# Moving the gate's clip of MLP 2 from VectorE to ScalarE, and half of the late w_out slices from MLP 2 into MLP 1

## The chip, the core and the metric

The kernel runs on one core of one Trainium2 chip. The metric is the time of one execution on the device in microseconds; lower is better. The core's engines are TensorE (PE: matmuls; PEld: its weight loads), VectorE (DVE), ScalarE (ACT), GpSimd (POOL) and SyncE (SP), whose queue issues all DMAs here. Each engine works through its own instructions in program order, so an instruction that waits holds up all that stand behind it.

## What is computed

Windowed attention feeds two MLPs in a row. The attention output becomes `x` with 3072 rows (tokens) and 512 columns; then

```python
def _moe_ref(x, w_in, w_out):            # MLP 1
    h = x @ w_in                         # 3072x512 @ 512x2048
    g = h - np.tanh(h)
    return g @ w_out                     # 2048x512

def _moe2_ref(x, w_in, w_out):           # MLP 2
    h = x @ w_in
    g = np.where(h >= 1, h, np.where(h <= -1, 0.0, (h + 1) ** 2 / 4))
    return g @ w_out
```

The weights arrive as 64-bit floats; the kernel rounds them to 32 bits itself, from their low and high words.

## The kernel before, in words

**Precision and rate.** Each factor is split into a high part (ACT copies it to `fp32r`, which rounds) and a low part (DVE subtracts the high part): `split_to`, lines 205 to 207. A product is then three matmuls (high by high, high by low, low by high), 128x128 by 128x512 each.

**MLP 1** is 96 steps (`NS`): 6 blocks of 512 tokens by 16 slices (`FC`) of 128 hidden columns. A step has 12 matmuls into `h` (`hidden`, line 464), the gate (`gate`: ACT Tanh, line 474, and DVE subtract, line 475) and, 16 steps behind (`LAG`), 12 matmuls into `acc` (`output`, `second`, line 499). The loop over steps `i` also calls what three tables hold for that step: `before` and `rounds` ahead of the step's matmuls, `behind` after its gate. `at_step` fills these tables by hand-set step numbers. The order in which the engines see the work is the order of these calls; nothing reorders it.

**The weights of MLP 2** are prepared inside MLP 1 by those tables: a slice is loaded into a `stage` tile (SP, line 121), turned into magnitude and low word on ACT (`round_act`, lines 133 and 136), put together by four DVE instructions (`round_rest`, lines 142, 143, 151 and 156), split (one ACT, one DVE instruction) and stored to DRAM (`wout`, two DMAs, line 244). Sixteen slices of `w_in` and the first eight of `w_out` (`EARLY_OUT`) are done in MLP 1, the `w_out` slices with one load tile (`stage3`) and one raw tile (`prep0`). The other eight (`LATE_OUT`) are done in MLP 2.

**MLP 2** is 24 calls of `quad(n)`: 3 superblocks of 1024 tokens by 8 pairs of hidden slices. A quad forms four 128x512 tiles of `h` with seven products (`mult`, 6 matmuls each, line 616) in place of eight, in the order 1, 2, 6, 5, 7, 4, 3, in two PSUM tiles: `qa` (bank `a`; two buffers in turn) and `qb` (banks `b` and `c`; one buffer, so that product 2 of a quad waits until the last gate of the quad before has read it). Partial sums leave `qa` by an ACT copy (`u`, line 632) ahead of the next product into it. The four gates (`gate2`, 96 in all) take `h` from a DVE add (line 643; one of the four reads `qa` directly). Line 646 clips to [-1, 1] on DVE, line 647 squares `0.5 t + 0.5` on ACT, and a last DVE instruction (`end`, line 650), put off to the next `gap`, takes the maximum with `h`.

Between the products stand four places, `gap(n, 0)` to `gap(n, 3)`. In each one output step of 12 matmuls is done: first the 17 left over from MLP 1 (`acc`; four each in quads 0 and 1, three each in quads 2 to 4, by `OLD_GAPS`), then those of MLP 2 (`acc_n`). `gap` splits the factors of the next output step as well (`ghi`, `glo`, `whi`, `wlo`). A quad has thus 90 matmuls with four output steps and 78 with three.

**The late slices before.** In quads 0 to 3, `late_out` does two slices per quad: round the first after gap 0, split it after gap 1, round the second after gap 2, split it after gap 3. The loads stand in the same quads: the first at the quad's start (line 730), the second after the first's split (line 756). In quad 3 four loads of activations for the next superblock (`x_load`, line 532) and eight loads of prepared weights (`load_out`, line 600) are issued ahead of the first. All these DMAs are in SP's one queue, with the `in<-win` loads (line 590) that feed the products.

Of the kernel before, what the change touches and what calls it, by code (L numbers as in the profile page):

```python
# [9 lines left out]
F32R = mybir.dt.float32r  # L10
# [3 lines left out]
AF = mybir.ActivationFunctionType  # L14
ALU = mybir.AluOpType
# [16 lines left out]
FC = DFF // 128  # L32
# [27 lines left out]
HALF = FC // 2  # L60
NSB = NB // 2
STREAM_IN, STREAM_OUT = 10, 8


OLD_GAPS = [(0, 1, 2, 3)] * 2 + [(0, 1, 2)] * 3

SPACE_A = (3, 4)
# [8 lines left out]
def tile_memory_attention_two_mlps(  # L76
# [9 lines left out]
    nc = tc.nc  # L86
# [13 lines left out]
    def slot(tag, name, dtype=F32):  # L100
        return slots.tile([128, 512], dtype, tag=tag, name=name)
# [3 lines left out]
    half = const.tile([128, 1], F32, name="half")  # L105
# [9 lines left out]
    def load_weights(phase, which, fc, tag=None):  # L115
        src = ((w1_in, w1_out), (w2_in, w2_out))[phase][which]
        if tag is None:
            tag = f"stage{loaded[0] % STAGES}"
            loaded[0] += 1
        stage = wide.tile([128, 512, 2], I32, tag=tag, name=f"stage{phase}{which}_{fc}")  # L120
        nc.sync.dma_start(out=stage, in_=src[fc])
        stage_t[phase, which, fc] = stage
# [3 lines left out]
    def round_act(phase, which, fc, part=None, tag=None):  # L126
        stage = stage_t[phase, which, fc]
        low, high = stage[:, :, 0], stage[:, :, 1]
        if part != 1:
            t = slot(tag or f"raw{which}_{fc}", f"raw{phase}{which}_{fc}")  # L130
            raw_t[phase, which, fc] = t

            nc.scalar.activation(out=t, in_=high.bitcast(F32), func=AF.Abs)
        if part != 0:

            nc.scalar.activation(out=low, in_=low.bitcast(U32), func=AF.Copy, scale=2.0 ** -29)
# [88 lines left out]
        for i, t in enumerate(parts_t.pop((q, m))):  # L225
            nc.sync.dma_start(out=win_d[q][:, 2 * m + i, :], in_=t.bitcast(F32))

    def prep_out_load(fc):
        load_weights(1, 1, fc, "stage3")

    def prep_out_act(fc):
        round_act(1, 1, fc, tag="prep0")

    def prep_out_rest(fc):
        round_rest(1, 1, fc)

    def prep_out_split(fc):
        hi, lo = slot("prep4", f"prepoh{fc}", F32R), slot("prep5", f"prepol{fc}", F32R)
        split_to(raw_t.pop((1, 1, fc)), hi, lo)
        parts_t["out", fc] = hi, lo  # L240

    def prep_out_store(fc):
        for i, t in enumerate(parts_t.pop(("out", fc))):
            nc.sync.dma_start(out=wout_d[fc][:, i, :], in_=t.bitcast(F32))
# [57 lines left out]
    scale = 1.0 / float(D) ** 0.5  # L302
# [147 lines left out]
    NS = len(steps)  # L450
# [186 lines left out]
    def gate2(n, r, c, src, plus=None):  # L637
        sb, q = n // HALF, n % HALF
        tag, g = take(f"g2_{n}_{r}{c}")
        gate_t[sb, r, q + c * HALF] = tag, g  # L640
        h = src
        if plus is not None:
            nc.vector.tensor_tensor(out=g, in0=src, in1=plus, op=ALU.add)  # L643
            h = g
        ttag, t = take(f"t2_{n}_{r}{c}")
        nc.vector.tensor_scalar(out=t, in0=h, scalar1=-1.0, scalar2=1.0, op0=ALU.max, op1=ALU.min)  # L646
        nc.scalar.activation(out=t, in_=t, func=AF.Square, scale=0.5, bias=half)  # L647

        def end():
            nc.vector.tensor_tensor(out=g, in0=h, in1=t, op=ALU.max)  # L650
            give(ttag)

        later.append(end)
# [64 lines left out]
    def quad(n):  # L718
        sb, q = n // HALF, n % HALF
        nxt = sb + 1  # L720
        more = nxt < NSB
        if more and q == HALF - 5:
            x_load(nxt)
        if n == 4:
            spare.extend(f"prep{i}" for i in range(6))
        if n == 3:
            for _ in range(STREAM_OUT // 2):
                load_out([spare.pop(0) for _ in range(2)])
        if n < 4:
            prep_out_load(LATE_OUT[2 * n])  # L730
        a = ps_h.tile([128, 512], F32, tag="h", name=f"qa{n}")
        pair = ps_a.tile([128, 2, 512], F32, tag="a", name=f"qb{n}")
        b, c = pair[:, 0, :], pair[:, 1, :]

        def mult(i, bank, first):
            if q == 0 or i not in (1, 2):
                xc[i] = xnext[i]
            product(n, i, bank, first)

        def then(i):  # L740
            if more and q == HALF - 1:
                x_split(nxt, i)

        def late_out(part):
            if n < 4:
                i, p = divmod(part, 2)
                fc = LATE_OUT[2 * n + i]
                if p == 0:
                    if i:
                        prep_out_store(LATE_OUT[2 * n])  # L750
                    prep_out_act(fc)
                    prep_out_rest(fc)
                else:
                    prep_out_split(fc)
                    if i == 0:
                        prep_out_load(LATE_OUT[2 * n + 1])

        mult(1, a, True)
        t1, u1 = take_copy(f"u1_{n}", a)
        mult(2, b, True)  # L760
        gate2(n, 0, 0, b, u1)
        give(t1)
        if q == 0:
            x_split(sb, 4) if sb == 0 else None
        gap(n, 0)
        late_out(0)
        if q == 0:
            x_split(sb, 3)
        if more and q == HALF - 4:
            x_sums(nxt, 0)  # L770
        if more and q == HALF - 2:
            x_split(nxt, 1)
        if more and q == HALF - 1:
            x_sum_last(nxt)
        mult(6, a, False)
        t2, u2 = take_copy(f"u2_{n}", a)
        mult(5, c, True)
        then(6)
        gap(n, 1)
        late_out(1)  # L780
        then(5)
        if more and q == HALF - 3:
            x_sums(nxt, 1)
        mult(7, a, False)
        t3, u3 = take_copy(f"u3_{n}", a)
        gate2(n, 1, 1, c, u3)
        give(t3)
        gap(n, 2)
        late_out(2)
        then(7)  # L790
        if more and q == HALF - 2:
            x_split(nxt, 2)
        mult(4, a, False)
        gate2(n, 1, 0, a)
        mult(3, c, False)
        gate2(n, 0, 1, c, u2)
        give(t2)
        gap(n, 3)
        late_out(3)
        if n < 4:  # L800
            prep_out_store(LATE_OUT[2 * n + 1])
        then(4)

    def out_fc_list(a, b):
# [2 lines left out]
    EARLY_OUT, LATE_OUT = out_fc_list(0, HALF), out_fc_list(HALF, FC)  # L807


    before, rounds, behind = {}, {}, {}  # L810

    def at_step(events, i, f, *args):
        assert i >= 0
        events.setdefault(int(i), []).append((i, f, args))


    for t in range(PER, NG + 1):
        k = t - PER
# [31 lines left out]
    for i, fc in enumerate(EARLY_OUT):  # L850
        p = PREP_IN + 5 + PREP_IN_EVERY * i
        at_step(before, p - 2, prep_out_load, fc)
        at_step(before, p, prep_out_act, fc)
        at_step(rounds, p, prep_out_rest, fc)
        at_step(before, p + 1, prep_out_split, fc)
        at_step(before, p + 2, prep_out_store, fc)


    def x_first():
# [28 lines left out]
    for j in range(PER):  # L888
        w = 0, 0, j
# [128 lines left out]
```

## Time and profile before

| what | value |
|---|---|
| median of 3 runs | 1146.48 us (1146.0 to 1146.83) |
| the profiled execution's own time | 1147.7 us |
| its span, first to last instruction | 1145.9 us |
| PE, DVE, ACT, POOL busy | 97%, 66%, 49%, 4% |
| mean granted TensorE clock over the span | 0.99 of full speed |
| DMA | 202.67 MB, mean 177 GB/s |
| MLP 1 steps, then quads of MLP 2 | quad 0 begins at 576.85 us |

The profile is one execution; its own time is 1.2 us above the median of the runs. Times in the rows count from the first instruction. "Idle before" is time in which an engine had nothing to run, and the name behind the arrow is what ended it. The granted clock is given as a share: 1.00 is 2.4 GHz, 0.50 is 1.2 GHz.

### The profile page before, as it was taken

The numbers are of one execution on the slowest core, as the hardware profiler recorded it, in microseconds if no ns is written. First come the engines' busy times: TensorE is split into PE (matmuls) and PEld (weight loads), VectorE is DVE, ScalarE is ACT, GpSimd is POOL, SyncE is SP. The second block draws the span as 40 slices with busy tenths as digits, with TensorE's granted clock in tenths as the row PEclk, the third lists the DMA queues.
The fourth block names the chain that finished last, engine by engine and source line by source line (L and its number), as shares of the span: only waits on it lengthen the run. The fifth ranks groups of instructions, "written<-read, shape, count | busy, mean of one in ns | idle before, by whom it ended". The sixth has DMA issues, their size and how long they took to land.

```text
span 1145.9 us, 20140 instructions
## 1 busy us (share of the span) xinstructions
PE 1107.9 (97%) x7799; PEld 897.1 (78%) x7799; DVE 759.2 (66%) x1340; ACT 556.0 (49%) x964; POOL 42.6 (4%) x38
## 2 busy tenths in 40 slices
PE   7899999999999999999999879999999999999998
PEld 3677888888888888888877658888888888888876
DVE  4799987887887887788567665565355564453522
ACT  3566665655656555566445443443334443333321
POOL 1132221000000000000000000000000000000000
PEclk9999999999999999999999989999999999999999
DMA  9996653626555454352244765657766557566364
GB/s 222 240 249 185 180 144 84 193 77 197 156 154 175 131 146 148 117 169 92 84 137 154 246 216 184 195 184 238 241 217 229 178 197 232 198 197 211 110 221 147
DMA packets 159648, 202.67 MB, mean 177 GB/s; under 512 B 61760, under 2 KB 86336, under 8 KB 159552
## 3 DMA queue, kind: packets, MB, share of 16 engines
q1 hardware_dynamic: 159552, 201.38, 56.5%
q8 instruction: 62, 1.02, 0.4%
q14 instruction: 34, 0.28, 0.1%
HBM read 165.68 MB, written 35.65 MB: 176 GB/s over the span
## 4 chain that ended last, share of the span: by engine, by line
PE 84%; DVE 7%; DMA 4%; ACT 3%; SPq 1%; issue 1%; DVEq 0%; ACTq 0%
PE h L464 23%; PE acc_n L499 22%; PE acc L499 19%; PE qa L616 9%; PE qb L616 7%; PE a L368 1%; DMA start<-qkv_t 1%; PE a L312 1%; DMA in<-win 1%; DVE g L650 1%; PE b L354 1%; DMA stage<-w_out 1%; DVE g L643 1%; DVE t L646 1%; DVE glo L207 1%
## 5 line engine op out<-in xcount | busy, mean ns | idle before, releaser
L207 DVE TENSOR_TENSOR glo<-g,ghi 128x512 fp32r<-128x512 f32 x192 | 132.6, 690 | 156.7 <-ACT ghi L206 105.7
L499 PE MATMUL acc_n<-ghi,out 128*128 128x512 f32 x768 | 194.2, 391 | 1.6 <-ACT yn L509 1.6
L499 PEld LDWEIGHTS acc_n<-ghi,out 128*128 128x128 f32 x768 | 143.3, 188 | 34.8 <-ACT yn L509 5.4
L206 ACT ACTIVATE ghi<-g 128x512 fp32r<-128x512 f32 x192 | 119.7, 624 | 80.9 <-PE acc L499 46.4
L616 PE MATMUL qa<-xc,in 128*128 128x512 f32 x576 | 148.0, 392 | 9.8 <-ACT u L632 9.7
L647 ACT ACTIVATE t<-t,half 128x512 f32<-128x512 f32 x96 | 69.5, 724 | 145.3 <-DVE t L646 145.0
L175 DVE TENSOR_TENSOR wlo<-raw,whi 128x512 fp32r<-128x512 f32 x192 | 134.7, 702 | 4.7 <-ACT whi L168 4.7
L616 PEld LDWEIGHTS qa<-xc,in 128*128 128x128 f32 x576 | 108.6, 189 | 33.9 <-ACT u L632 11.5
L168 ACT ACTIVATE whi<-raw 128x512 fp32r<-128x512 f32 x192 | 120.6, 628 | 23.9 <-PE acc L499 16.5
L643 DVE TENSOR_TENSOR g<-qb,u 128x512 f32<-128x512 f32 x72 | 49.7, 690 | 101.6 <-ACT u L632 77.6
L474 ACT ACTIVATE g<-h 128x512 f32<-128x512 f32 x96 | 57.2, 596 | 121.4 <-PE h L464 88.0
L616 PE MATMUL qb<-xc,in 128*128 128x512 f32 x432 | 111.3, 393 | 3.7 <-DVE g L643 3.7
L499 PE MATMUL acc<-ghi,whi 128*128 128x512 f32 x384 | 110.7, 403 | 2.5 <-ACT y L509 1.5
L499 PE MATMUL acc<-ghi,wlo 128*128 128x512 f32 x384 | 106.3, 391 | 0.4 <-DVE wlo L175 0.2
L499 PE MATMUL acc<-glo,whi 128*128 128x512 f32 x384 | 105.7, 389 | 0.0
L499 PE MATMUL acc_n<-glo,out 128*128 128x512 f32 x384 | 105.5, 389 | 0.0
L464 PE MATMUL h<-xh,whi 128*128 128x512 f32 (+2 forms) x392 | 105.4, 391 | 0.0
L632 ACT ACTIVATE u<-qa 128x512 f32<-128x512 f32 x72 | 42.8, 595 | 127.9 <-PE qa L616 127.9
L464 PE MATMUL h<-xl,whi 128*128 128x512 f32 (+2 forms) x392 | 103.9, 387 | 0.2 <-DVE xl L399 0.2
L464 PE MATMUL h<-xh,wlo 128*128 128x512 f32 (+2 forms) x392 | 103.7, 386 | 0.0
L616 PEld LDWEIGHTS qb<-xc,in 128*128 128x128 f32 x432 | 81.6, 190 | 21.9 <-DVE g L643 5.0
L475 DVE TENSOR_TENSOR g<-h,g 128x512 f32<-128x512 f32 x96 | 66.1, 688 | 47.8 <-ACT g L474 47.6
(89 smaller groups left out, 1327.3 us busy)
## 6 DMA issues: line engine op xcount, KB each, us to landing
out<-wout SPq DMA_DIRECT2D x192, 256.0 KB, 3.0
in<-win SPq DMA_DIRECT2D x168, 256.0 KB, 3.6
stage<-w_in SPq DMA_DIRECT2D x32, 512.0 KB, 5.2
stage<-w_out SPq DMA_DIRECT2D x32, 512.0 KB, 4.2
k<-qkv_t SPq DMA_DIRECT2D x80, 128.0 KB, 4.8
v<-qkv_t SPq DMA_DIRECT2D x80, 128.0 KB, 3.4
win<-preph SPq DMA_DIRECT2D x32, 256.0 KB, 3.0
yd<-y SPq DMA_DIRECT2D x24, 256.0 KB, 2.7
```

The source lines that it names most:

```text
L168: nc.scalar.activation(out=hi, in_=r, func=AF.Copy)
L175: nc.vector.tensor_tensor(out=lo, in0=r, in1=hi.bitcast(F32), op=ALU.subtract)
L206: nc.scalar.activation(out=hi, in_=src, func=AF.Copy)
L207: nc.vector.tensor_tensor(out=lo, in0=src, in1=hi.bitcast(F32), op=ALU.subtract)
L464: nc.tensor.matmul(hp, w[:, kc * 128:(kc + 1) * 128], x[:, kc, n0:n1], start=j == 0 and kc == 0, stop=j == 2 and kc == KC - 1,)
L474: nc.scalar.activation(out=g, in_=hp, func=AF.Tanh)
L475: nc.vector.tensor_tensor(out=g, in0=hp, in1=g, op=ALU.subtract)
L499: nc.tensor.matmul(acc_t[dm], w[:, dm * 128:(dm + 1) * 128], g, start=first and j == 0, stop=last and j == 2,)
L616: nc.tensor.matmul(bank, w[:, k * 128:(k + 1) * 128], z[k], start=first and j == 0 and k == 0, stop=j == 2 and k == 1, skip_group_check=True,)
L632: nc.scalar.activation(out=t, in_=bank, func=AF.Copy)
L643: nc.vector.tensor_tensor(out=g, in0=src, in1=plus, op=ALU.add)
L647: nc.scalar.activation(out=t, in_=t, func=AF.Square, scale=0.5, bias=half)
```

## The change

Three things change, in the code below.

1. **The gate.** DVE's clip is gone. ACT does Relu of `0.5 h + 0.5`, then Square, and the last DVE instruction does `max(min(t, 1), h)` in one.
2. **Four late slices move into MLP 1.** Slices 0 to 3 of `LATE_OUT` are rounded at steps 88, 90, 92 and 94 and split one step later, with loads two steps ahead, each into a `stage` tile of its own, and with two sets of prepared tiles in turn.
3. **The other four stay in quads 0 to 3, one per quad:** rounded after gap 0, split after gap 2, stored after gap 3. Their loads are issued at steps 94 (three) and 95 (one), ahead of quad 0.

```diff
+LATE_ALONE = 4
@@ gate2
-        nc.vector.tensor_scalar(out=t, in0=h, scalar1=-1.0, scalar2=1.0, op0=ALU.max, op1=ALU.min)
-        nc.scalar.activation(out=t, in_=t, func=AF.Square, scale=0.5, bias=half)
+        nc.scalar.activation(out=t, in_=h, func=AF.Relu, scale=0.5, bias=half)
+        nc.scalar.activation(out=t, in_=t, func=AF.Square)
         def end():
-            nc.vector.tensor_tensor(out=g, in0=h, in1=t, op=ALU.max)
+            nc.vector.scalar_tensor_tensor(out=g, in0=t, scalar=1.0, in1=h, op0=ALU.min, op1=ALU.max)
@@ quad
-        if n < 4:
-            prep_out_load(LATE_OUT[2 * n])
...
         def late_out(part):
-            if n < 4:
-                i, p = divmod(part, 2)
-                fc = LATE_OUT[2 * n + i]
-                if p == 0:
-                    if i:
-                        prep_out_store(LATE_OUT[2 * n])
-                    prep_out_act(fc)
+            i = n + LATE_ALONE
+            if i < HALF:
+                fc = LATE_OUT[i]
+                if part == 0:
+                    prep_out_act(fc, i)
                     prep_out_rest(fc)
-                else:
-                    prep_out_split(fc)
-                    if i == 0:
-                        prep_out_load(LATE_OUT[2 * n + 1])
+                elif part == 2:
+                    prep_out_split(fc, i)
+                elif part == 3:
+                    prep_out_store(fc)
@@ the tables of MLP 1
+    for i, fc in enumerate(LATE_OUT):
+        p = NS - FC + 8 + 2 * i
+        if i < LATE_ALONE:
+            at_step(before, p - 2, prep_out_load, fc, i)
+            at_step(before, p, prep_out_act, fc, i)
+            at_step(rounds, p, prep_out_rest, fc)
+            for k, f, args in ((1, prep_out_split, (fc, i)), (2, prep_out_store, (fc,))):
+                at_step(before if p + k < NS - 1 else behind, min(p + k, NS - 1 + 0.1 * k), f, *args)
+        else:
+            at_step(behind, NS - 2 if i < 2 * LATE_ALONE - 1 else NS - 1, prep_out_load, fc, i - LATE_ALONE)
```

TensorE's instructions stand in the same order in both kernels. Three places on other engines follow, before and now. Lines from 65 on have moved: 121, 133, 168, 206, 244, 590, 600, 632, 643 of before are 122, 134, 169, 207, 246, 592, 602, 634, 645 now.

SP's queue in quad 3, before; the `out` rows are the last two of eight loads of prepared weights, behind four of activations:

```order
L600 DMA out_0_3_0_7695<-wout_109 128x512
L600 DMA out_0_3_1_7696<-wout_109 128x512
L121 DMA stage_7_7699<-w_out 128x1024
L590 DMA in_3_7717<-win_96 128x512
L590 DMA in_4_7719<-win_96 128x512
L590 DMA in_5_7768<-win_96 128x512
L590 DMA in_6_7770<-win_96 128x512
L121 DMA stage_15_7796<-w_out 128x1024
L244 DMA wout_107<-prepoh_7792 128x512
L244 DMA wout_107<-prepol_7793 128x512
```

The same place now:

```order
L602 DMA out_0_3_0_7712<-wout_109 128x512
L602 DMA out_0_3_1_7713<-wout_109 128x512
L592 DMA in_3_7732<-win_96 128x512
L592 DMA in_4_7734<-win_96 128x512
L592 DMA in_5_7783<-win_96 128x512
L592 DMA in_6_7785<-win_96 128x512
L592 DMA in_0_7851<-win_97 128x512
L592 DMA in_1_7853<-win_97 128x512
L592 DMA in_2_7865<-win_97 128x512
L246 DMA wout_115<-prepoh_7841 128x512
L246 DMA wout_115<-prepol_7842 128x512
```

The two loads of raw `w_out` slices (`stage`) are gone from this quad; they stand at the end of MLP 1.

ACT in quad 3 before, from the copy of the quad's first product (`u_3`) to the copy ahead of its fifth, with the rounding of a late slice (`raw`, `stage`) between:

```order
L632 ACTIVATE u_3_7709<-qa_7701 128x512
L647 ACTIVATE t_3_00_7723<-t_3_00_7723,half 128x512
L206 ACTIVATE ghi_7726<-g_6880 128x512
L168 ACTIVATE whi_91_7730<-raw_11_2355 128x512
L133 ACTIVATE raw_7_7747<-stage_7_7699 128x512
L136 ACTIVATE stage_7_7699<-stage_7_7699 128x512
L632 ACTIVATE u_3_7760<-qa_7701 128x512
```

The same place now:

```order
L634 ACTIVATE u_3_7724<-qa_7716 128x512
L648 ACTIVATE t_3_00_7738<-g_3_00_7736,half 128x512
L649 ACTIVATE t_3_00_7738<-t_3_00_7738 128x512
L207 ACTIVATE ghi_7741<-g_6906 128x512
L169 ACTIVATE whi_91_7745<-raw_11_2355 128x512
L134 ACTIVATE raw_15_7762<-stage_15_7137 128x512
L137 ACTIVATE stage_15_7137<-stage_15_7137 128x512
L634 ACTIVATE u_3_7775<-qa_7716 128x512
```

Relu and Square stand where Square stood; the rounding is in the same place, of a slice that was loaded at step 95.

DVE in quad 2 before, from the second gate's add (`g_2_11`) to the ends of the last two gates; the next quad's product 2 waits for the add `g_2_01`:

```order
L643 TENSOR_TENSOR g_2_11_7605<-qb_7501,u_2_7603 128x512
L646 TENSOR_SCALAR t_2_11_7607<-g_2_11_7605 128x512
L207 TENSOR_TENSOR glo_7611<-g_6832,ghi_7610 128x512
L175 TENSOR_TENSOR wlo_90_7616<-raw_10_2233,whi_90_7614 128x512
L650 TENSOR_TENSOR g_2_11_7605<-g_2_11_7605,t_2_11_7607 128x512
L142 TENSOR_SCALAR raw_14_7633<-raw_14_7633 128x512
L143 TENSOR_SCALAR raw_14_7633<-raw_14_7633 128x512
L151 SCALAR_TENSOR_TENSOR raw_14_7633<-stage_14_7595,raw_14_7633 128x512
L156 ISA raw_14_7633<-stage_14_7595,raw_14_7633 128x1024
L646 TENSOR_SCALAR t_2_10_7651<-qa_7500 128x512
L643 TENSOR_TENSOR g_2_01_7662<-qb_7501,u_2_7559 128x512
```

The same place now:

```order
L645 TENSOR_TENSOR g_2_11_7631<-qb_7533,u_2_7629 128x512
L208 TENSOR_TENSOR glo_7637<-g_6847,ghi_7636 128x512
L176 TENSOR_TENSOR wlo_90_7642<-raw_10_2233,whi_90_7640 128x512
L652 SCALAR_TENSOR_TENSOR g_2_11_7631<-t_2_11_7633,g_2_11_7631 128x512
L208 TENSOR_TENSOR prepol_7658<-raw_7_7578,prepoh_7657 128x512
L645 TENSOR_TENSOR g_2_01_7683<-qb_7533,u_2_7591 128x512
```

Two clips and the four roundings of the second slice are gone from between the two adds; one subtraction of the late slice's split (`prepol`) has come in.

## Rows read from the trace of the kernel before

**Rows 1.** Page, part 1: busy time of each engine, share, instructions.

```profile
PE 1107.9 (97%) x7799; PEld 897.1 (78%) x7799; DVE 759.2 (66%) x1340; ACT 556.0 (49%) x964; POOL 42.6 (4%) x38
```

**Rows 2.** Who PE waited for, whole span: us in total, times, longest.

```profile
PE qa L616 <- ACT u L632: 9.7, 3, 8.5
...
PE qb L616 <- DVE g L643: 3.7, 3, 2.2
```

**Rows 3.** Busy time by stretch (length, engines, clock, DMA): one step, quads 0 to 4.

```profile
565.97:571.41 5.44, 5.44 (x25) 4.50 (x24) 1.99 (x3) 1.87 (x3) 0.00 (x0) 1.00 0.01 3
576.85:600.11 23.26, 21.43 (x91) 16.58 (x90) 15.90 (x28) 12.30 (x22) 0.00 (x0) 1.00 0.54 169
600.11:623.03 22.92, 21.33 (x91) 16.62 (x90) 16.81 (x30) 12.03 (x21) 0.00 (x0) 1.00 0.56 173
623.03:642.45 19.42, 18.67 (x79) 14.33 (x78) 14.28 (x25) 12.03 (x21) 0.00 (x0) 1.00 0.52 168
642.45:674.94 32.49, 21.75 (x79) 17.01 (x78) 16.66 (x30) 11.08 (x19) 0.00 (x0) 0.79 0.72 250
674.94:694.25 19.31, 18.02 (x79) 14.56 (x78) 14.08 (x25) 7.85 (x14) 0.00 (x0) 1.00 0.37 119
```

**Rows 4.** Timeline in quad 3: start, length, engine, instruction, [idle before <- releaser].

```profile
651.09 6.85 SPq L600 DMA_DIRECT2D out<-wout  x8
...
658.30 0.33 SPq L121 DMA_DIRECT2D stage<-w_out  x1
...
664.38 0.66 ACT L133 ACTIVATE raw<-stage 128x512 f32<-128x512 f32 x1 [12.18 <-DMA stage<-w_out]
...
666.13 2.93 PE L616 MATMUL qa<-xc,in 128*128 128x512 f32 x6 [8.50 <-ACT u L632]
```

**Rows 5.** Busy time by stretch, as rows 3, inside that wait.

```profile
660.00:665.00 5.00, 0.00 (x0) 0.00 (x0) 0.00 (x0) 0.62 (x2) 0.00 (x0) 0.50 1.05 393
```

**Rows 6.** Timeline in quad 1, columns as rows 4.

```profile
611.26 0.66 ACT L133 ACTIVATE raw<-stage 128x512 f32<-128x512 f32 x1 [2.31 <-DMA stage<-w_out]
...
613.02 1.65 PE L616 MATMUL qa<-xc,in 128*128 128x512 f32 x6 [1.00 <-ACT u L632]
```

**Rows 7.** Timeline where quad 2 ends and quad 3 begins.

```profile
644.27 0.69 DVE L156 CUSTOM_DVE_ANT_0 raw<-stage,raw 128x1024 uint16<-128x1024 uint16 x1
644.88 0.69 DVE L646 TENSOR_SCALAR t<-qa 128x512 f32<-128x512 f32 x1
645.48 0.68 DVE L643 TENSOR_TENSOR g<-qb,u 128x512 f32<-128x512 f32 x1
...
646.22 2.93 PE L616 MATMUL qb<-xc,in 128*128 128x512 f32 x6 [2.24 <-DVE g L643]
```

**Rows 8.** Timeline in quad 0.

```profile
586.69 1.33 PE L499 MATMUL acc<-ghi,whi 128*128 128x512 f32 x4 [1.52 <-ACT y L509]
```

**Rows 9.** Groups by line and shape: count | busy us, mean ns | idle before.

```profile
L206 ACT ACTIVATE ghi<-g 128x512 fp32r<-128x512 f32 x192 | 119.7, 624 | 80.9 <-PE acc L499 46.4 <-PE acc_n L499 34.2
L647 ACT ACTIVATE t<-t,half 128x512 f32<-128x512 f32 x96 | 69.5, 724 | 145.3 <-DVE t L646 145.0 <-DMA yd<-y 0.3
...
L650 DVE TENSOR_TENSOR g<-g,t 128x512 f32<-128x512 f32 x72 | 49.3, 685 | 0.6 <-ACT t L647 0.6
L151 DVE SCALAR_TENSOR_TENSOR raw<-stage,raw 128x512 int32<-128x512 int32 x64 | 44.3, 692 | 2.1
L646 DVE TENSOR_SCALAR t<-g 128x512 f32<-128x512 f32 x72 | 30.8, 427 | 2.5
...
L646 DVE TENSOR_SCALAR t<-qa 128x512 f32<-128x512 f32 x24 | 16.4, 685 | 0.0
```

**Rows 10.** Busy time by stretch: step 84 and step 88 of MLP 1.

```profile
517.02:522.46 5.44, 5.44 (x26) 4.50 (x25) 5.41 (x10) 3.41 (x7) 0.00 (x0) 1.00 0.31 118
538.77:544.21 5.44, 5.44 (x25) 4.50 (x24) 3.10 (x6) 2.54 (x5) 0.00 (x0) 1.00 0.45 148
```

**Rows 11.** Who ACT waited for, 700 to 1120 us: us in total, times, longest.

```profile
ACT u L632 <- PE qa L616: 119.0, 48, 4.3
```

More of the change, by code (lines that the diff above doesn't have):

```diff
@@ L226, in prep_store, with prep_out_load, prep_out_act, prep_out_split @@
             nc.sync.dma_start(out=win_d[q][:, 2 * m + i, :], in_=t.bitcast(F32))
[L228 to L232, printed above, removed]
+    def prep_out_load(fc, i=3):
+        load_weights(1, 1, fc, f"stage{i}")
+    def prep_out_act(fc, i=0):
+        round_act(1, 1, fc, tag=f"prep{i % 2}")
     def prep_out_rest(fc):
         round_rest(1, 1, fc)
-    def prep_out_split(fc):
-        hi, lo = slot("prep4", f"prepoh{fc}", F32R), slot("prep5", f"prepol{fc}", F32R)
+    def prep_out_split(fc, i=0):
+        w = 4 - 2 * (i % 2)
+        hi, lo = slot(f"prep{w}", f"prepoh{fc}", F32R), slot(f"prep{w + 1}", f"prepol{fc}", F32R)
         split_to(raw_t.pop((1, 1, fc)), hi, lo)
@@ L799, in quad @@
         late_out(3)
-        if n < 4:
-            prep_out_store(LATE_OUT[2 * n + 1])
         then(4)
```

## The prediction

> **What bounds the kernel now.** I read the busy shares first: PE is busy 97% of the span [rows 1], so only what makes PE wait, or run at the lower clock, can give much back. DVE at 66% and ACT at 49% matter where PE waits for them. The list of PE's waits names two lines of MLP 2 above the rest: 9.7 us for ACT's copy `u`, 8.5 of them in one wait, and 3.7 us in three waits for DVE's add [rows 2]. Where these lie I read from stretches of one quad each [rows 3]. The first row there is a step of MLP 1 without a wait: 24 matmuls in 5.44 us, 0.2267 us each. At this pace a quad of 90 matmuls takes 20.40 us and one of 78 takes 17.68. Against that, quad 0 (23.26) loses 2.86 us, quad 1 (22.92) 2.52, quad 2 (19.42) 1.74, quad 3 (32.49) 14.81, quad 4 (19.31) 1.63: 23.56 us in all. The lost time is thus in the five quads that still carry late slices or their aftermath, with quad 3 far ahead, where the mean granted clock was 0.79 as well [rows 3].
>
> Why quad 3 loses so much stands in its timeline [rows 4]. SP issues eight loads of prepared weights from 651.09 on, and only at 658.30 the raw `w_out` slice; ACT's rounding of that slice waits for it until 664.38, 12.18 us. The copy `u` stands behind the rounding on ACT, PE's next product behind `u`: 8.50 us. During it the DMA engines are full, 393 GB/s at a share of 1.05, and the granted clock goes down to 0.50, the 1.2 GHz level [rows 5]; the six matmuls after the wait take 2.93 us against 1.36 at the full pace [rows 4]. The other large wait of quad 3 is at its start, with a different cause [rows 7]: DVE does the last rounding of a late slice (644.27), a clip (644.88) and only then the add that frees `qb` (645.48), and PE's product 2 starts at 646.22 after 2.24 us, again slow (2.93 us). Beyond these two waits (10.74 us) quad 3 loses 4.07 us, which I put down to the two slow restarts, half to each: about 10.5 us hang on the late load and 4.3 on DVE's queue.
>
> **The change part by part.**
>
> *Loads ahead.* The four loads for quads 0 to 3 are issued at steps 94 and 95, ahead of quad 0. Then ACT's rounding finds its slice landed in quads 1 to 3. In quad 1 the same wait (2.31 us on ACT) costs PE 1.00 us and a slow start [rows 6]; in quad 3 it costs the 10.5. In front of them in SP's queue now stand the stores of slices 2 and 3; behind them stand loads of `in` tiles for quads 0 and 1, the first of which quad 1 needs 23 us later. I price that at nothing; the cover is those 23 us, and without it a late tile would cost quad 1 a wait of its length.
>
> *One slice per quad.* In quads 0 to 3 the second rounding goes: two clips of 0.427 and two bit operations of 0.692 on DVE (L151 for both, as the nearest row), 2.24 us, and with the split's 0.685 2.9 us of DVE time per slice; on ACT three instructions of about 0.62 [rows 9]. That rounding lay after gap 2, right ahead of the add for which PE waited [rows 7]. With it and the clip of `qa` (0.685 [rows 9]) gone, one subtraction (0.69) comes in. So the add of 645.48 moves 2.24 + 0.69 - 0.69 = 2.2 us ahead, plus 0.43 for the clip of the gate before it: 2.7 us against the wait of 2.24. So the wait goes, with some 0.4 us to spare. The DVE queue also holds up the starts of quads 1, 2 and 4. I take all of it as gone except 0.5 us over quads 1 to 4, an estimate: the margin is a fraction of a DVE instruction, in three places. The first rounding of each quad stays after gap 0, where PE has 12 + 12 matmuls (5.4 us) ahead of it before it needs `u`.
>
> *Four slices in MLP 1.* Each puts 2.24 us on DVE at an even step (88, 90, 92, 94) and 0.69 at the next, and 1.3 and 0.62 us on ACT. Step 88 has DVE busy for 3.10 of its 5.44 us, step 84 for 5.41, and in both PE is busy for all 5.44 [rows 10]. 3.10 + 2.24 = 5.34 stays under what step 84 already carries without a loss. I price it at 0; if DVE were the bound there, the four slices would cost at most 4 x 2.9 = 11.7 us less the idle 2.3 us of each of eight steps, which is below zero again.
>
> *The gate.* Per gate DVE loses a clip (0.427, or 0.685 from PSUM). Its last instruction becomes one with two operations and two inputs: the nearest row of that kind is L151, 0.692 against 0.685 now, so +0.01. ACT does Relu (0.724, with the bias, as L647) and Square (0.624, without one, as L206) where it did one of 0.724 [rows 9]. What stands behind Square on ACT thus starts 0.724 + 0.624 - 0.427 - 0.724 = 0.20 us later when the gate's add is the last thing it waits for. In quad 0 this lies on PE's path: the eviction of the last sums of MLP 1's fifth block, for which PE waits 1.52 us [rows 8], stands behind two splits that follow Square. So quad 0 loses 2.86 + 0.2 = 3.06 us. Elsewhere ACT waits for PE ahead of the copies `u`: 119.0 us in 48 waits, 2.5 us each [rows 11]. That is the cover for the 0.62 us of ACT time per gate; without it the price is the second rival's.
>
> The Trainium skill speaks against this edit: ScalarE: Activation LUTs, section Rules for kernel authors, says that relu, max and min belong on VectorE and not on ScalarE. This trace agrees on the price of one instruction (0.427 against 0.724 us [rows 9]); the rule does not look at which engine others wait for. What would come of it is the second rival.
>
> *The sum.* Before: 23.56 us lost. After: 3.06 in quad 0, 0.5 in quads 1 to 4. The gain is 20.0 us. Against the profiled execution's own 1147.7 us that gives 1127.7; its time is 1.2 above the median of the runs, and from the median, 1146.48, it gives **1126.5**.
>
> Bounds: if quad 0 does not get its 0.2 and nothing stays in the others, and the third wait for DVE's add (3.7 - 2.24 leaves 1.5 for two, of which quad 4 has one) goes too, the gain is 21.2 and the time 1125.3. If each of quads 1 to 4 keeps 0.7 us, it is 17.7 and 1128.8.
>
> **The rivals.**
>
> *First: only the late loads mattered.* The add ahead of product 2 still comes too late, because the longer chain on ACT (Relu, Square, then `ghi`, for which DVE's `glo` waits) delays what stands ahead of the add on DVE. Then only the DMA part goes: 10.5 in quad 3, 1.0 in quad 1, less 0.2: 11.3 us, 1135.2. For it speaks that my margin at that place is only 0.4 us; against it that ACT's part of the chain grew by 0.2 us only, while 2.7 us left DVE's queue.
>
> *Second, slower: ACT becomes the bound in every quad.* Two of a quad's four gates have a copy `u` soon behind them on ACT, for which PE waits. If the extra 0.62 us of each landed on PE in all 24 quads, that is 29.8 us, and 1126.5 + 29.8 = 1156.3. It decides from the point where ACT is less than 0.62 us ahead at those copies; it is 2.5 us ahead on the mean now [rows 11], and ACT is busy for 7.85 of 19.31 us in quad 4 [rows 3]. So it is unlikely. With half of it on the path the gain would be mostly eaten: 1141.4.
>
> *Third: the change does not do what it says,* because the DMA engines and not the place in the queue make the tile late. Quad 3's first twelve loads (4 MB) still run at 393 GB/s [rows 5], some 10.5 us, and now the `in` tiles for quad 4 come behind them, as they did. If one of these became the late thing, a wait of up to 8.5 us would return: 1126.5 + 8.5 = 1135.0. Against it: quad 4 needs the first such tile in its third product, 23 us after quad 3 begins.
>
> **How the numbers follow.** Forecast 0.78, first rival 0.12, second 0.06, third 0.04. The forecast's own range is 1125.3 to 1128.8, and from below I allow 1 us more. The forecast alone does not hold 8 in 10 with its own spread, so the range reaches to the first and third rivals: 1124.3 to 1135.5. About 0.2% (2.3 us) is what a measurement of this kernel can tell from no change. Forecast, first and third rival are all faster by more. Of the second I give 0.01 to the partial case within 0.2% and 0.05 to slower. So faster 0.94, same 0.01, slower 0.05; I move 0.01 from faster to same for what I have not thought of.
>
> **What would show it.** Right: no wait of PE for ACT's `u` above 0.5 us in quads 1 to 3; ACT's rounding waits for no `w_out` load there; quads 1 to 4 at 20.4, 17.7, 17.7 and 17.7 us; a granted clock of 1.00 in all of them; quad 0 still near 23.4; steps 88 to 95 at 5.44 us with DVE above 5 in the even ones. Wrong: quads 3 and 4 begin with a wait for DVE's add (first rival); waits of PE for `u` in quads 5 to 23, or quads of over 20.6 us there (second); a wait of PE for an `in` tile in quad 4 (third). A step between 88 and 95 of over 5.5 us would mean that MLP 1 did not hide its slices.

## The result and the profile after

The changed kernel takes 1125.43 us (median of 5 runs, 1124.01 to 1127.78) against 1146.18 before (5 runs): a ratio of 0.9822, 95% interval 0.9807 to 0.9838, 20.75 us less. Measured once more (changed_again), it was 0.9824 (0.9808 to 0.9841). The forecast was 1126.5, a gain of 20.0.

Quad by quad, in the view of [rows 3] (length, PE, PEld, DVE, ACT and POOL busy with counts, granted clock, DMA share, GB/s), quads 0 to 4 after:

```profile
576.84:600.30 23.46, 21.46 (x91) 16.58 (x90) 13.34 (x22) 15.42 (x27) 0.00 (x0) 1.00 0.62 208
600.30:620.70 20.40, 20.40 (x91) 16.89 (x90) 12.22 (x20) 12.57 (x23) 0.00 (x0) 1.00 0.37 119
620.70:638.38 17.68, 17.68 (x79) 14.64 (x78) 11.06 (x19) 10.97 (x20) 0.00 (x0) 1.00 0.32 98
638.38:656.08 17.70, 17.70 (x79) 14.62 (x78) 10.93 (x19) 11.60 (x21) 0.00 (x0) 1.00 0.97 338
656.08:673.78 17.70, 17.70 (x79) 14.61 (x78) 10.68 (x18) 8.67 (x16) 0.00 (x0) 1.00 0.45 161
```

Quads 1 to 4 run at the full pace, at a granted clock of 1.00; quad 3, which took 32.49 us [rows 3], takes 17.70, though its DMA engines are busier than before (338 GB/s against 250). Of these five only quad 0 still loses, 23.46 - 20.40 = 3.06 us.

Who PE waited for, over the whole span (us in total, times, longest); the lines of [rows 2] are gone, these are what is left of MLP 2:

```profile
PE acc_n L501 <- ACT yn L511: 2.4, 5, 0.6
...
PE acc L501 <- ACT y L511: 1.7, 1, 1.7
...
PE acc L501 <- DVE wlo L176: 0.2, 1, 0.2
```

Groups of the new gate and of ACT's first rounding instruction (count | busy us, mean ns | idle before):

```profile
L649 ACT ACTIVATE t<-t 128x512 f32<-128x512 f32 x96 | 60.7, 632 | 3.0
L648 ACT ACTIVATE t<-g,half 128x512 f32<-128x512 f32 x72 | 52.1, 724 | 69.5 <-DVE g L645 69.5
L652 DVE SCALAR_TENSOR_TENSOR g<-t,g 128x512 f32<-128x512 f32 x72 | 49.3, 685 | 2.3 <-ACT t L649 2.3
L134 ACT ACTIVATE raw<-stage 128x512 f32<-128x512 f32 x64 | 42.4, 663 | 0.0
```

L134 never waited for a slice to land (0.0; it was 12.18 us in quad 3 alone [rows 4]). Relu takes 724 ns, Square 632, and the last DVE instruction 685, as long as the one that it replaces [rows 9].

**How times are compared below.** The profiled executions reach quad 0 between 574.1 and 576.9 us. Most of this spread arises in the first 50 us, where no edit touches anything. So beside the timed ratio I give the time from quad 0's first matmul to the end of the span, which leaves that out. It comes from one execution of each kernel: from quad 23 on, where before and loads_ahead are the same program, they take 81.33 and 80.88 us, so differences up to 0.5 us in the last column say nothing. The medians come from four rounds, and each ratio is to the kernel before in the same round.

| kernel | median us | ratio to before (95%) | quad 0 to end, us |
|---|---|---|---|
| before | 1146.18 | 1 | 569.05 |
| changed | 1125.43 | 0.9822 (0.9807 to 0.9838) | 549.16 |
| changed_again | 1125.63 | 0.9824 (0.9808 to 0.9841) | 549.02 |
| gate_only | 1144.21 | 0.9993 (0.9983 to 1.0002) | 567.67 |
| slices_only | 1126.27 | 0.9830 (0.9815 to 0.9844) | 549.18 |
| load_first | 1141.47 | 0.9957 (0.9940 to 0.9974) | 564.90 |
| one_load_back | 1137.80 | 0.9929 (0.9913 to 0.9946) | 560.13 |
| loads_ahead | 1132.94 | 0.9894 (0.9874 to 0.9915) | 554.33 |
| act_one_more | 1133.65 | 0.9907 (0.9881 to 0.9934) | 556.19 |
| act_three_more | 1239.51 | 1.0823 (1.0801 to 1.0844) | 662.61 |
| evict_first | 1120.89 | 0.9791 (0.9774 to 0.9808) | 543.67 |
| evict_shift | 1121.15 | 0.9784 (0.9769 to 0.9798) | 543.48 |
| evict_shift_clip | 1120.52 | 0.9780 (0.9765 to 0.9796) | 543.98 |

Changed_again is the changed kernel unaltered, run beside evict_shift and evict_shift_clip:

> The changed kernel itself once more, on the same chip as the two others, so that their differences are taken on one chip: 1125.4 within 1.5 us.

By the last column the change is worth 19.89 us (569.05 - 549.16).

### The profile page after: what moved, and what is told of

Same layout as the page of the kernel before. It is cut to its first block, busy times and chain, and to the rows that moved or that the text cites. A ratio compares the mean times of both kernels' runs of the same rounds, so it can differ in the third digit from the quotient of the medians.

```text
span 1126.0 us, 20104 instructions
## 1 busy us (share of the span) xinstructions
PE 1101.8 (98%) x7799; PEld 895.6 (80%) x7799; DVE 713.8 (63%) x1244; ACT 614.8 (55%) x1060; POOL 42.5 (4%) x38
## 4 chain that ended last, share of the span: by engine, by line
PE 93%; DVE 3%; ACT 2%; issue 1%; DMA 0%; SPq 0%; DVEq 0%; ACTq 0%
PE h L466 23%; PE acc L501 23%; PE acc_n L501 22%; PE qa L618 11%; PE qb L618 8%; PE a L370 1%; PE a L314 1%; PE b L356 1%; PE start_tx L889 1%; PE b L390 1%; DVE g L652 1%; ACT e L344 0%; DMA start<-qkv_t 0%; DVE yn L513 0%; ACT t L648 0%
## 5 line engine op out<-in xcount | busy, mean ns | idle before, releaser
L169 ACT ACTIVATE whi<-raw 128x512 fp32r<-128x512 f32 x192 | 120.6, 628 | 23.2 <-PE acc L501 16.6
L648 ACT ACTIVATE t<-g,half 128x512 f32<-128x512 f32 x72 | 52.1, 724 | 69.5 <-DVE g L645 69.5
```

Of the source, the lines that this page charges most:

```text
L169: nc.scalar.activation(out=hi, in_=r, func=AF.Copy)
L648: nc.scalar.activation(out=t, in_=h, func=AF.Relu, scale=0.5, bias=half)
```

## Experiments: which part does it

### The gate alone

```diff
 # the kernel before, and:
-        nc.vector.tensor_scalar(out=t, in0=h, scalar1=-1.0, scalar2=1.0, op0=ALU.max, op1=ALU.min)
-        nc.scalar.activation(out=t, in_=t, func=AF.Square, scale=0.5, bias=half)
+        nc.scalar.activation(out=t, in_=h, func=AF.Relu, scale=0.5, bias=half)
+        nc.scalar.activation(out=t, in_=t, func=AF.Square)
...
-            nc.vector.tensor_tensor(out=g, in0=h, in1=t, op=ALU.max)
+            nc.vector.scalar_tensor_tensor(out=g, in0=t, scalar=1.0, in1=h, op0=ALU.min, op1=ALU.max)
```

> The kernel before with the new gate alone; all eight late slices stay in quads 0 to 3, two each, with their loads where they were. Theory (three separate parts: late loads, DVE's queue ahead of the add, 0.2 us more on ACT's chain at evictions): quad 3's wait of 8.5 us for ACT's u stays. The clips of 0.43 and 0.69 us leave DVE's queue ahead of the add, so PE's waits for it at the starts of quads 3 and 4 shrink by 1.1 us each, from 2.2 and 1.3 to 1.1 and 0.2. Five evictions cost 0.2 us more. Gain 2 us: 1144. Rival (the gate is what frees the starts, and the slices matter only through their loads): gain 6 us or more, 1140. Rival (ACT becomes the bound): slower than 1147.

Measured: 0.9993, not to be told from no change; 1.4 us from quad 0 on, where I had expected 2. One part of the expectation failed: PE's waits for the add at the starts of quads 3 and 4 were 1.79 and 1.39 us, not 1.1 and 0.2. Quads 1 and 2 did become shorter (21.85 and 18.93 us against 22.92 and 19.42), but the timeline of quad 3's large wait (columns as in [rows 4]) shows what became of that:

```profile
654.65 0.33 SPq L121 DMA_DIRECT2D stage<-w_out  x1
...
660.68 0.66 ACT L133 ACTIVATE raw<-stage 128x512 f32<-128x512 f32 x1 [12.72 <-DMA stage<-w_out]
...
662.43 2.07 PE L616 MATMUL qa<-xc,in 128*128 128x512 f32 x4 [10.41 <-ACT u L632]
```

The wait is 10.41 us in place of 8.50. Counted from quad 0, PE arrives 3.4 us earlier, but the slice lands only 1.5 us earlier, and the wait ends when it lands: 1.9 of the 3.4 us are given back in waiting.

### The slices alone

```diff
 # the changed kernel, with the old gate: the diff above, reversed
```

> The changed kernel with the old gate (clip on DVE, one Square on ACT). Theory: quads 1 and 2 at 20.4 and 17.7 us as in the changed kernel; the two clips return 1.1 us to DVE ahead of the add, of which the 0.2 us of margin takes a part, so quads 3 and 4 begin with waits of about 0.9 us and slow restarts, and quad 5 with 0.2; the evictions go back from 0.44 to 0.24 us. Against the 1125.4 of the changed kernel 2.5 us more: 1128. Rival (the gate's part is nothing, since DVE is not the bound): 1124.4, that is 1 us less than the changed kernel, for the evictions.

Measured: 0.9830, and 549.18 us from quad 0 on against 549.16 with the new gate. I had expected 2.5 us more than the changed kernel, and there is nothing. PE's waits for the add, in its list of waits:

```profile
PE qb L618 <- DVE g L645: 0.4, 2, 0.2
```

Two waits of 0.2 us, where I had expected 0.9 each at two starts. With the slower starts behind them, quads 3 to 5 lose more than the list shows (view of [rows 3]):

```profile
636.65:654.75 18.10, 18.02 (x80) 14.56 (x78) 12.69 (x23) 9.35 (x16) 0.00 (x0) 1.00 0.97 340
654.75:672.94 18.19, 17.98 (x79) 14.56 (x78) 12.56 (x22) 7.34 (x13) 0.00 (x0) 1.00 0.43 148
672.94:693.83 20.89, 20.69 (x91) 16.81 (x90) 12.47 (x22) 9.16 (x15) 0.00 (x0) 1.00 0.77 249
```

The changed kernel takes 17.70, 17.70 and 20.43 us there, so the new gate is worth 0.40 + 0.49 + 0.46 = 1.35 us at these three starts. It gives that back at five other places: quads 0, 9, 13, 17 and 21, which end a block's sums, are 0.21 to 0.23 us longer each with it, 1.13 in all. The net is nothing that can be measured.

Why the two clips delay the add so little is seen where quad 2 ends and quad 3 begins (timelines, other rows left out). First the changed kernel:

```profile
636.44 0.69 DVE L208 TENSOR_TENSOR glo<-g,ghi 128x512 fp32r<-128x512 f32 x1 [1.98 <-ACT ghi L207]
...
637.65 0.68 DVE L652 SCALAR_TENSOR_TENSOR g<-t,g 128x512 f32<-128x512 f32 x1
...
638.25 0.69 DVE L208 TENSOR_TENSOR prepol<-raw,prepoh 128x512 fp32r<-128x512 f32 x1
...
638.86 0.69 DVE L645 TENSOR_TENSOR g<-qb,u 128x512 f32<-128x512 f32 x1
...
639.75 1.53 PE L618 MATMUL qb<-xc,in 128*128 128x512 f32 x6
```

Then slices_only, with the clip of `qa` ahead of the add:

```profile
634.50 0.69 DVE L208 TENSOR_TENSOR glo<-g,ghi 128x512 fp32r<-128x512 f32 x1 [1.31 <-ACT ghi L207]
...
636.92 0.68 DVE L648 TENSOR_SCALAR t<-qa 128x512 f32<-128x512 f32 x1
637.52 0.68 DVE L645 TENSOR_TENSOR g<-qb,u 128x512 f32<-128x512 f32 x1
...
638.25 1.67 PE L618 MATMUL qb<-xc,in 128*128 128x512 f32 x6
```

DVE waits for ACT's `ghi` between the two adds, 1.98 us without the first clip and 1.31 with it: that clip (0.43 us) stood in the wait and cost nothing. The clip of `qa` does stand ahead of the add, but the shorter chain on ACT brings `glo` 0.2 us earlier. So the add ends 0.2 us ahead of PE's product 2 in the changed kernel (639.55 against 639.75), and some 0.2 us late in slices_only.

### The loads alone

```diff
 # the kernel before, all late slices still in quads 0 to 3, two each, and:
-    def prep_out_load(fc):
-        load_weights(1, 1, fc, "stage3")
+    def prep_out_load(fc, i=3):
+        load_weights(1, 1, fc, f"stage{i}")
...
-        if n < 4:
-            prep_out_load(LATE_OUT[2 * n])
...
                     prep_out_rest(fc)
+                    if n < 2:
+                        prep_out_load(LATE_OUT[2 * n + i + 4], 2 * n + i)
                 else:
                     prep_out_split(fc)
-                    if i == 0:
-                        prep_out_load(LATE_OUT[2 * n + 1])
...
+    for i in range(4):
+        at_step(behind, NS - 2, prep_out_load, LATE_OUT[i], i)
```

> The kernel before (old gate, all eight late slices in quads 0 to 3, two each) with the loads alone moved ahead: four at step 94 into four stage tiles, the other four in quads 0 and 1, each as soon as its stage tile is free. Theory: every wait of ACT for a raw w_out slice goes, and with it what PE lost for it in quads 1, 2 and 3, 1.5 + 0.9 + 10.6 = 13 us; the waits of 2.2 and 1.3 us for DVE's add at the starts of quads 3 and 4 stay, since both slices are still rounded there: 1133. Rival (the slices' work on ACT and DVE was the cause, the loads were late only because of it): under 6 us gained, above 1139. Rival (loads were all of it): 1127.

Measured: 1132.94, as the theory had it; 569.05 - 554.33 = 14.7 us from quad 0 on. No wait of PE for `u` is left. What is left is DVE's add, as expected:

```profile
PE qb L616 <- DVE g L643: 4.3, 3, 2.2
```

So of the change's 19.9 us the loads make 14.7. The remaining 5.2 I put down to one rounding less per quad, since the gate makes nothing of them on balance (slices_only); no run has that part alone. The split is less sure than the sum: this profiled execution was the fastest of four, and by the medians the loads make 12.3 of 20.8 us.

### One load, put first and put back

```diff
 # load_first: the kernel before, in quad(n)
+        if n < 4:
+            prep_out_load(LATE_OUT[2 * n])
         if more and q == HALF - 5:
             x_load(nxt)
...
             for _ in range(STREAM_OUT // 2):
                 load_out([spare.pop(0) for _ in range(2)])
-        if n < 4:
-            prep_out_load(LATE_OUT[2 * n])
```

> The kernel before with one edit: in quad 3 the load of the raw w_out slice is issued ahead of the four activation loads and the eight loads of prepared weights, not behind them. Theory (the place in the queue makes the 8.5 us wait): ACT's wait for the slice falls from 12.2 us to about 1, PE's wait for u to under 1, quad 3 loses about 10 us less: 1136. All other waits of quads 0 to 4 stay. Rival (the DMA engines are full, so the wait moves to another tile): PE waits for an in tile or the activations later in quad 3 or 4, and the time stays above 1142.

Measured: 0.9957, 1141.47 us, 4.2 us less from quad 0 on; I had expected 1136. PE's wait for `u` in quad 3 is gone, as expected. But the wait came back at the start of quad 4, in a form that neither expectation named:

```profile
661.31 0.33 SPq L121 DMA_DIRECT2D stage<-w_out  x1
...
667.33 0.66 ACT L133 ACTIVATE raw<-stage 128x512 f32<-128x512 f32 x1 [7.40 <-DMA stage<-w_out]
...
670.98 0.68 DVE L643 TENSOR_TENSOR g<-qb,u 128x512 f32<-128x512 f32 x1
...
671.71 1.65 PE L616 MATMUL qb<-xc,in 128*128 128x512 f32 x3 [8.67 <-DVE g L643]
```

It is quad 3's second slice: its load stands in the program behind the first one's split, and so behind the twelve transfers and `in` tiles. It lands at 667.3, and through ACT's and DVE's queues holds up the add. I read this as the same cause, a raw slice behind the burst, of which my edit had moved one of two. The opposite edit, in the changed kernel, has only one slice to move:

```diff
 # one_load_back: the changed kernel; the last late load is not issued at step 95, and in quad(n)
...
                 load_out([spare.pop(0) for _ in range(2)])
+            prep_out_load(LATE_OUT[7], 3)
```

> The changed kernel with the load of quad 3's slice put back into quad 3, behind the twelve other loads; the rest as changed. Theory: ACT's rounding waits for the slice again, PE waits for u 6 to 8.5 us and restarts at the lower clock: 1133 to 1136. Rival (what mattered was the number of slices per quad, not this load): within 1 us of the changed kernel's 1125.4.

Measured: 0.9929, and 560.13 us from quad 0 on, 11.0 more than the changed kernel. The wait is back in its old form:

```profile
637.23 2.26 SPq L534 DMA_DIRECT2D a<-yd  x4
...
639.54 8.52 SPq L602 DMA_DIRECT2D out<-wout  x8
...
648.41 0.33 SPq L122 DMA_DIRECT2D stage<-w_out  x1
...
654.42 0.66 ACT L134 ACTIVATE raw<-stage 128x512 f32<-128x512 f32 x1 [12.34 <-DMA stage<-w_out]
...
656.17 1.22 PE L618 MATMUL qa<-xc,in 128*128 128x512 f32 x2 [9.37 <-ACT u L634]
```

One DMA of 512 KB in the wrong place of SP's queue costs 11 us, 9.4 in the wait and the rest in the slow start behind it (by the medians 12.4, on different chips). Most of its lateness lies ahead of its issue: SP starts on the twelve loads at 637.23 and comes to the slice at 648.41, 11.2 us later. From issue to landing it then takes 6.0 us; the slice that load_first issued ahead of the burst took 3.8.

## Experiments: what the gate costs, and where ACT's slack ends

In the four evictions of MLP 2 that come inside quads, PE waits longer than before. First the kernel before, then the changed one, at the same eviction:

```profile
779.47 2.23 PE L499 MATMUL acc_n<-ghi,out 128*128 128x512 f32 x8 [0.24 <-ACT yn L509]
```

```profile
758.73 2.25 PE L501 MATMUL acc_n<-ghi,out 128*128 128x512 f32 x8 [0.44 <-ACT yn L511]
```

The 0.20 us is as long as the lengthening of the gate's chain (Relu and Square against clip and Square) that I had put down for quad 0 alone. To see how much more of it the kernel bears, the gate was given more ACT instructions that change nothing:

```diff
 # act_one_more: the changed kernel, and (act_three_more: three of them)
         nc.scalar.activation(out=t, in_=t, func=AF.Square)
+        nc.scalar.activation(out=t, in_=t, func=AF.Copy)
```

> The changed kernel with one more ACT instruction in every gate, a copy of t onto itself (0.62 us, values unchanged), between Square and what follows. Theory (ACT is ahead of PE by 2.5 us at its copies, and the chain shows only at the five evictions and at the three quads that follow a quad of three output steps): 0.65 us more at each of the five, and about 0.5 with a restart at each of the three: 4 to 6 us more than the changed kernel, 1130. Rival (ACT is the bound in every quad): 24 quads by two gates by 0.62 us, 30 us more, 1155.

> The changed kernel with three more such copies in every gate, 1.9 us of ACT time and of chain. Theory: at the five evictions 2 us each, at the three quad starts 2 us each with slow restarts, and nothing in the others, since ACT then works about 17 of 20.4 us per quad: 15 to 22 us more, 1141 to 1147. Rival (bound in every quad): 24 by two by 1.9 us, 90 us more, above 1200. This is to find where ACT's slack ends.

Measured: one more costs 7.0 us (556.19 against 549.16), above the theory's 4 to 6, and 8.2 by the medians (1133.65; the profiled execution was the fastest of four). Three more cost 113 us, where the theory had 15 to 22: that theory was wrong, and the price is above its rival's 90. Each quad from 5 on takes 23.2 us or more, where it took 20.4. Who PE waited for with one more:

```profile
PE acc_n L501 <- ACT yn L511: 5.0, 5, 1.1
...
PE acc L501 <- ACT y L511: 2.4, 1, 2.4
...
PE acc_n L501 <- ACT ghi L207: 1.1, 2, 0.7
PE qb L618 <- DVE g L645: 1.0, 3, 0.4
```

and with three more:

```profile
PE acc_n L501 <- ACT ghi L207: 35.7, 28, 4.0
PE acc_n L501 <- ACT yn L511: 17.3, 5, 4.2
...
PE qa L618 <- ACT u L634: 3.6, 3, 2.6
```

With one more, the evictions and three quad starts wait, as the theory says, and two waits for `ghi` appear. With three, ACT's `ghi`, the high part for the next output step, is late 28 times. It stands behind the gate's chain on ACT. The copies `u`, from whose idle time of 2.5 us [rows 11] I had judged ACT's slack, are late three times. So the slack is at another instruction, and it runs out between one and three instructions of 0.62 us more per gate; the change itself used one. The list's waits (77 us of MLP 2 for `ghi`, `yn`, `whi`, `y`, `u` and the add, against 4.4 in the changed kernel) do not make up the whole 113. The other 41 us are longer matmuls: from quad 0 on PE is busy for 581.1 us against 539.8, at a mean granted clock of 0.96 against 1.00.

## A faster version

In the changed kernel the copies that empty the sums out of PSUM stand on DVE behind `glo`, which waits for ACT's `ghi`, and behind the put-off ends of the gates. In evict_first, where an output step is the last of its block, these come after the copies; in quad 0 a split of activations moves behind the gap as well:

```diff
 # evict_first: the changed kernel, in gap; prepare puts the low parts of step k + 1 into late
...
+            late = None
+            if n < NSB * HALF and (what % FC if kind == "old" else what[2]) == FC - 1:
+                late = []
             if k + 1 < len(queue) and ready(queue[k + 1], n, g):
-                prepare(k + 1)
-            flush()
+                prepare(k + 1, late)
+            if late is None:
+                flush()
...
             at[0] += 1
+            for f in late or ():
+                f()
         flush()
 # and in quad
-        if q == 0:
-            x_split(sb, 4) if sb == 0 else None
         gap(n, 0)
+        if q == 0:
+            x_split(sb, 4) if sb == 0 else None
```

> The changed kernel with the order at an eviction turned: where an output step is the last of its block, the copies of the sums out of PSUM stand on DVE ahead of the next step's low-part subtractions and of the put-off ends of the gates, and in quad 0 the split of the activations comes after it. Theory (the evictions are late because on DVE they stand behind instructions that wait for the gate's chain on ACT): the waits of PE for ACT's y and yn, 1.7 us in quad 0 and four times 0.44 (0.6 to 0.9 with the restart), go: 4 to 5.5 us less than the changed kernel, 1120.5. Rival (the copies themselves are the wait, about 2.4 us after the last matmul): nothing gained, 1125.

Measured: 0.9791, 1120.89 us, 5.5 us less from quad 0 on than the changed kernel. What is left of the waits in MLP 2:

```profile
PE acc L501 <- DVE wlo L176: 0.7, 1, 0.7
...
PE acc_n L501 <- ACT yn L511: 0.6, 1, 0.6
```

The four waits of 0.44 and the one of 1.7 us are gone; the last eviction, behind the last quad, was left as it was. Quads 9, 13, 17 and 21 fall from 21.30 to 20.40 us by the order alone; quad 0 falls from 23.46 to 21.58, and there no run parts the order from the moved split. Evict_shift moves the four late slices from quads 0 to 3 into quads 1 to 4:

```diff
-        if n == 4:
+        if n == 5:
             spare.extend(f"prep{i}" for i in range(6))
...
-            i = n + LATE_ALONE
-            if i < HALF:
+            i = n - 1 + LATE_ALONE
+            if LATE_ALONE <= i < HALF:
```

> The kernel evict_first with the four late slices of MLP 2 in quads 1 to 4 in place of 0 to 3. Theory: quad 0 has the split of the activations and a late slice's rounding in one place, and PE still waits 0.74 us there for a low part of the weights with its restart; without the slice that goes, and quads 1 to 4 hide one slice each: 1 us less than evict_first's 1120.9, so 1120. Rival (quad 4, which has the activations' sums and an eviction, cannot hide it): the same or more, 1121 to 1122.

Measured: 0.9784, 543.48 us from quad 0 on against 543.67: the rival was right. The wait for `wlo` is of the same size and has gone from quad 0 to quad 4 (at 664 us), which has the activations' sums to do:

```profile
PE acc L501 <- DVE wlo L176: 0.7, 1, 0.7
```

Evict_shift_clip is evict_shift with the old gate:

> The kernel evict_shift with the old gate (clip on DVE, one Square on ACT). Theory (the gate's edit is worth nothing once the slices are out of the way, as slices_only showed): within 1 us of evict_shift. Rival (with the evictions repaired, the 0.2 us that Relu adds to ACT's chain is gone, so the new gate's relief of DVE shows alone): 1 to 2 us slower than evict_shift, by waits for DVE's add at the starts of quads 3 to 5.

Measured: 0.9780 against 0.9784, intervals that overlap almost wholly; 543.98 against 543.48 us. The theory holds: with the slices out of the way it makes no measurable difference which engine clips, though quads 3 to 5 are 0.7 us longer with the old gate, so the rival's direction may be real at a size below what the runs can tell. All three versions are faster than the kernel before, and are not to be told from each other. The intervals of evict_shift and evict_shift_clip also lie clear of that of changed_again, run beside them. Evict_first's just meets that of the changed kernel (up to 0.9808, from 0.9807); its gain over the changed kernel rests on the waits that are gone and the 5.5 us from quad 0 on.

## Why the prediction was right, step by step

- **The number.** The forecast was 1126.5, a gain of 20.0 us from the medians; measured were 1125.43 and 20.75, in the profiled executions 19.89. That the two sums agree so closely is in part luck, as the terms below show.
- **What bounds the kernel.** Right. Quads 0 to 4 lost 23.56 us and lose 3.1, a gain of 20.46. Outside them quad 5 gained 0.47 (20.90 to 20.43 us), with a wait of 0.2 us at its start, and the four quads with an eviction lost 0.96.
- **Loads ahead.** Right in its mechanism, which load_first, one_load_back and loads_ahead show from three sides, and short in its size. I had put 10.5 us on the load in quad 3 and 1.0 in quad 1. In loads_ahead quads 1, 2 and 3 are 1.6, 1.0 and 12.3 us shorter; quad 2 I had not priced. About 1.6 us of quad 3's 12.3 is the slow start at its beginning, which I had given to DVE's queue (4.3 us there): with the loads ahead PE waits as long there (2.17 against 2.24 us) but runs on at the full clock (1.65 us for six matmuls and 1.07 for the next four, against 2.93 and 1.42). Why it does is not known, so this part may not be the loads' own.
- **One slice per quad.** The starts of quads 3 and 4 are free, as forecast, with the 0.2 us of spare time that the trace shows in place of the 0.4 that I worked out. Its share, by difference, is 5.2 us, by the medians 8.
- **The gate as part of that.** Half wrong. Of the two clips that I took off DVE's queue, "plus 0.43 for the clip of the gate before it" brought nothing. I added up instructions on DVE's queue and did not ask whether DVE would wait there anyway. It does, 1.98 us for `ghi`. The other, the 0.685 of the clip of `qa`, brought its time less the 0.2 us by which Relu delays `ghi`. Slices_only shows what is left: 1.35 us over the starts of quads 3 to 5, which the evictions take back.
- **The gate's price.** The 0.2 us in quad 0 came out exactly: 3.06 us forecast, 3.06 measured. But the same sum of durations applies at every eviction. I had kept the rest of the gate's chain covered by ACT's idle time ahead of `u`, and it is not: four more quads pay 0.2 us each (waits of 0.24 become 0.44). The sum had this term at nothing.
- **The 0.5 us left over in quads 1 to 4.** Not there: 20.40, 17.68, 17.70 and 17.70 us. These 0.5 us, the 0.47 of quad 5 and the 0.96 of the evictions nearly cancel, so that the sum of 20.0 us met 19.89.
- **Four slices in MLP 1 at no cost.** Right. Steps 90 and 94 in the view of [rows 10]:

```profile
549.62:555.06 5.44, 5.44 (x25) 4.51 (x24) 5.18 (x10) 3.69 (x7) 0.00 (x0) 1.00 0.03 11
...
571.38:576.84 5.46, 5.46 (x25) 4.51 (x24) 4.74 (x8) 3.01 (x5) 0.00 (x0) 1.00 1.01 364
```

  DVE at 5.18 of 5.44 us leaves PE without a gap, as step 84 had before [rows 10]. DVE was busy for 4.7 to 5.2 us in the four steps, not above 5 in each as I had written.
- **The rivals.** The first would have needed DVE's add to stay late; it did not. The second did not come, and it named the wrong instruction (`u`), but its mechanism is real: act_three_more, with three ACT instructions more per gate, is it, at 8% slower. The third, a late `in` tile in quad 4, did not come either: quad 4 takes 17.70 us. The Trainium skill's rule (ScalarE: Activation LUTs, Rules for kernel authors) would have left relu on VectorE. Here that would have cost nothing that can be measured (slices_only, evict_shift_clip): the rule was no reason against the kernel's gain, since the gain is not the gate's.

## What to carry to other kernels

Look where in its queue a transfer stands that an engine waits for: here one slice behind twelve other loads cost 11 us, and nothing when it was issued ahead of them. All such transfers have to be moved; moving one of two brought 4.2 us of the 14.7. Before a removed instruction is counted as time won on a queue, look whether the queue waits behind it anyway. And an engine's slack is to be read at each instruction that others wait for, not from its mean idle time at one of them.

## What the runs showed of the hardware that I had not expected

After a wait of about 2.2 us at the start of quad 3 PE restarted in different ways. In the kernel before, six matmuls took 2.93 us [rows 7], at a granted clock of 0.50. In load_first and loads_ahead, after 2.19 and 2.17 us, they took 1.66 and 1.65, at 1.00. After the four waits of 8.5 to 10.4 us they took 2.92 to 2.93 us each time. After four waits of 1.3 to 1.9 us at the starts of quads 3 and 4 (in the kernel before, gate_only and loads_ahead) they took 1.65 to 1.67 us. What else decides at 2.2 us was not taken apart.
